# One weight block of a decode kernel brought as sixteen uneven small transfers instead of eight even ones

## The chip, the cores and the metric

The kernel runs on one core of one Trainium2 chip. The metric is the device time of one execution in microseconds. Three runs of the kernel before gave 675.16, 675.23 and 676.45 us, so the median is 675.23 us.

## The reference

The model is one decode step with two parts on the same input `x` (2 rows of 448), mixed by a gate:

```python
def reference(A_x, A_k_cache, A_v_cache, A_wq, A_wo, B_x, B_w1, B_w2, gate_w):
    ...
    x = A_x
    g = _sigmoid((x * gate_w).sum(-1, keepdims=True))
    a = _A_ref(x, A_k_cache, A_v_cache, A_wq, A_wo)   # attention, 16 heads of 256, 4096 cached keys, then wo
    b = _B_ref(x, B_w1, B_w2)                         # relu(x @ w1) @ w2, 448 -> 1792 -> 448
    return g * a + (1 - g) * b
```

All is float32. The two caches hold 2 x 16 x 4096 x 256 values each and are read once; they are 268 MB of the 289.6 MB that the kernel reads.

## The kernel before

The work is cut into 32 units, one for each batch row and head. A unit's keys and values are one transfer of 128 rows of 65,536 bytes, which goes into one of three slots in on-chip memory. All large loads are issued from the SyncE queue (SP), in program order: `wq` and two units ahead of the loop, thirty units in the loop (L126 to L131), each when its slot is free, and then the function `late`. TensorE makes a unit's scores, VectorE the maximum and the weighted sums of the values, ScalarE the exponentials.

`late` (L141) brings the last weights, in this order on one queue:

- `w1` (128 rows of 23,296 bytes, one transfer) into slot 2, as soon as the last unit there has been used up;
- `w1x`, the part of w1 that lies apart: the last 448 columns of w1's 128 rows. It is packed as 64 rows of 3,584 bytes and goes to partitions 0 to 63, in eight transfers of 8 rows (L144 to L146). A transfer's rows lie four partitions apart;
- `w2` (128 rows of 25,088 bytes);
- `wo` in five transfers of 128 rows into slot 0 (14, 10, 4, 3 and 1 blocks of 448 columns, `CUTS`), as soon as slot 0 is free.

TensorE waits for w1 and for all of `w1x` in front of the first product of the second part (L336), then for w2 (L357), and then for each piece of wo in front of the blocks that it holds (L375). The last product of the program uses the last blocks of wo. After it VectorE copies the result (`res`, L397) and SP stores it (`out`, L402).

A transfer is carried by several of the core's 16 DMA engines, each with its share of the rows and, behind them, a 4-byte write that raises the transfer's semaphore; a semaphore at 16 says that all has landed. In the text below such a write is called a mark. DMA engines take their shares in the order in which the transfers were issued.

Of the kernel before, what the change touches and what calls it, by code (L numbers as in the profile page):

```python
# [8 lines left out]
P, HP = 128, 64  # L9
G = 4  # L10
R = P // G
SLOTS = 3
NB = 2
ENGINES = ("tensor", "vector", "scalar", "gpsimd", "sync")


class Program:
# [6 lines left out]
    def __init__(self, nc):  # L24
        self.nc = nc
        self.code = {e: [] for e in ENGINES}
        self.count = dict.fromkeys(ENGINES, 0)

# [11 lines left out]
    def emit(self, block, sems):  # L40
        def run(name):
            def body(e):
                seen = {}
                for kind, a, b in self.code[name]:
                    if kind == "loop":
                        with e.Fori(0, a) as i:
                            b(e, i)
                        continue
                    for who, n in b:
                        if seen.get(who, 0) < n:  # L50
                            e.wait_ge(sems[who], n)
                            seen[who] = n
                    if kind == "op":
                        a(e).then_inc(sems[name], 1)
                    else:
                        a(e)
            return body

        for name in ENGINES:
            getattr(block, name)(run(name))  # L60


def take(e, sem, n=1):
    e.wait_ge(sem, n)
    e.sem_inc(sem, -n)  # L65


def gated_mix_decode(nc, xg, kv, wq, w1, w1x, w2, wo, out):
# [13 lines left out]
    RB = R // B  # L82
    HB = H // NB
    UB = U // NB
    HH = HB // G
# [5 lines left out]
    def sbuf(name, *shape):  # L91
        return nc.alloc_sbuf_tensor(name, [*shape], F32).ap()

    def bank(name, n=CW):
        return nc.alloc_psum_tensor(name, [P, n], F32).ap()

    NO = NB * HH * J
    CUTS = (0, NO - 18, NO - 8, NO - 4, NO - 1, NO)
    TAIL = 8
    names = [*ENGINES, "xg", "w1x", "w2", *(f"wo{k}" for k in CUTS[1:]), "query", "score", "top", "prob", "room",  # L100
             *(f"land{s}" for s in range(SLOTS)), *(f"free{s}" for s in range(SLOTS)), "out"]
    sem = {n: nc.alloc_semaphore(n) for n in names}
    land = [sem[f"land{s}"] for s in range(SLOTS)]
    free = [sem[f"free{s}"] for s in range(SLOTS)]
    pr = Program(nc)
    pe, dve, act, pool, sp = ENGINES

# [8 lines left out]
    def load(s, src, signal, lo=0, hi=None):  # L116
        hi = src.shape[1] if hi is None else hi
        return lambda e: e.dma_start(slot[s][:, lo:hi], src[:, lo:hi]).then_inc(signal, 16)  # L118
# [15 lines left out]

    W1, WX = w1.shape[1], w1x.shape[2]
    w1_sb, w1x_sb = slot[2][:, :W1 + WX], slot[2][:, W1:W1 + WX]
    w2_sb = slot[2][:, W1 + WX:W1 + WX + NF * D]

    def late(e):  # L141
        take(e, free[2])
        load(2, w1, land[2])(e)
        for k in range(8):  # L144
            o = k // 4 * 4 * 8 + k % 4
            e.dma_start(w1x_sb[o:o + 4 * 7 + 1:4], w1x[k]).then_inc(sem["w1x"], 16)  # L146
        e.dma_start(w2_sb, w2).then_inc(sem["w2"], 16)
        take(e, free[0])
        for lo, hi in zip(CUTS, CUTS[1:]):
            load(0, wo, sem[f"wo{hi}"], lo * D, hi * D)(e)  # L150
        take(e, free[1])

    pr.raw(sp, late)

    ident = sbuf("ident", P, P)
# [56 lines left out]
    W = 2 * KF * DH  # L212
    WQ = wq.shape[1] // NB
    wide = sbuf("wide", P, CW)
    pr.raw(pe, lambda e: take(e, land[2], 16))
    busy = [(), ()]
    for i in range(NB):
        w = slot[2][:, i * WQ:(i + 1) * WQ]
        for c in range(KC):
            for g in range(G):  # L220
                r = rows_of(c, g // 2)
                at = g * W + c * CW if c < KF else G * W + g % 2 * CW
# [7 lines left out]
        for s in range(2):  # L230
            dst = qt.rearrange("p t (i g s b) -> p i s t g b", i=NB, g=G, s=2)[:, i, s]
            src = pt[:, ::RB].rearrange("p (s t g b) -> p s t g b", s=2, t=T, g=G)[:, s]
# [100 lines left out]
    hs = wide[:, :FG]  # L333
    hr = sbuf("hr", P, NF, R)
    ph, pt = pw[3], pw[2]
    pr.raw(pe, lambda e: (take(e, land[2], 16), e.wait_ge(sem["w1x"], 16 * 8)))  # L336
    half = (W1 + WX // 2) // 2
    for c in range(KC):
        for g in range(G):
            j, i = divmod(g, 2)  # L340
            at = i * half + (j * KF + c if c < KF else 2 * KF + i * j) * FG
# [26 lines left out]
    n = NO - TAIL  # L368
# [17 lines left out]
    at = 0  # L386
# [80 lines left out]
```

## Time and profile before

| | before |
|---|---|
| median of 3 runs | 675.23 us (675.16 to 676.45) |
| span of the profiled execution | 674.6 us |
| DMA packets, bytes | 6180, 289.66 MB |
| queue of the large loads (q1), share of 16 engines | 99.3% |
| VectorE busy | 341.5 us (51%) |
| TensorE busy | 224.6 us (33%) |
| issue of the eight `w1x` transfers on SP | 5.48 us, from 619.67 |
| landing of the last-but-one piece of wo, which ends TensorE's last wait | 671.59 us |
| result copied, store issued | 672.75, 673.05 us |

The profiled execution has its span and no time of its own beside it; the span lies 0.6 us under the median of the runs. The times in the tables count from the first instruction of the span. The share of a DMA queue is the time that its packets took, over 16 engines and the whole span. In a table of stretches, the column "DMA share" is the same for that stretch: 1.00 is all 16 engines at work, 0.50 is eight. Packets that overlap a little on one engine can lift it over 1.

### The profile page before, as it was taken

What the parts mean: (1) busy time and instruction counts of PE and PEld (TensorE: products, weight loads), DVE (VectorE), ACT (ScalarE), POOL (GpSimd) and SP (SyncE); (2) the same over time, 40 slices, a digit from 0 to 9 for tenths busy, and PEclk for the clock granted to TensorE, in tenths of its full rate; (3) what the DMA queues carried; (4) which work ended last, traced back from release to release, by engine and by line L of the source; (5) the groups of instructions that cost most, each with busy time, mean ns of one, the idle gap of its engine ahead of it and who ended that gap; (6) DMA issues with size and microseconds to landing.
All of it is one profiled execution on the core that took longest, in us unless ns stands there. A gap on an engine that the chain in (4) does not pass through costs nothing. (4 is left out here: it accounts for less than half of the span.)

```text
span 674.6 us, 4166 instructions
## 1 busy us (share of the span) xinstructions
PE 224.6 (33%) x1323; PEld 67.0 (10%) x1323; DVE 341.5 (51%) x571; ACT 59.7 (9%) x121; POOL 0.7 (0%) x6
## 2 busy tenths in 40 slices
PE   0643221333332123333322333333222333321277
PEld 0210000001001000100100010010001001000022
DVE  0006566544556664455566545455665544657652
ACT  0020001001000100100010010000001001000010
POOL 0000000000000000000000000000000000000000
PEclk9975567667655666765566676665567666556688
DMA  9999999999999999999999999999999999999997
GB/s 381 428 435 436 436 435 435 435 435 435 435 431 435 435 435 435 435 431 435 435 435 435 435 435 435 435 435 435 435 435 435 435 431 427 435 427 435 400 444 316
DMA packets 6180, 289.66 MB, mean 429 GB/s; under 512 B 992, under 2 KB 1120, under 8 KB 1440
## 3 DMA queue, kind: packets, MB, share of 16 engines
q1 hardware_dynamic: 6032, 289.60, 99.3%
q8 instruction: 3, 0.05, 0.0%
q10 hardware_dynamic: 144, 0.01, 0.0%
q14 instruction: 1, 0.01, 0.0%
HBM read 289.54 MB, written 0.06 MB: 429 GB/s over the span
## 5 line engine op out<-in xcount | busy, mean ns | idle before, releaser
L274 DVE SCALAR_TENSOR_TENSOR slot<-slot,prob 128x1024 f32<-128x1024 f32 x256 | 295.9, 1222 | 65.1 <-DVEq L65 65.1
L251 PE MATMUL ps<-slot,query 128*32 128x512 f32 x1024 | 190.8, 909 | 404.4 <-PEq L65 404.3
L270 DVE TENSOR_REDUCE nm<-ps 128x1024 f32 (+1 forms) x32 | 39.2, 1225 | 230.8 <-DVEq L65 230.8
L251 PEld LDWEIGHTS ps<-slot,query 128*32 128x32 f32 x1024 | 54.7, 158 | 539.1 <-issue 539.0
L263 ACT ACTIVATE prob<-ps,nm 128x1024 f32<-128x1024 f32 x32 | 35.6, 1113 | 385.0 <-ACTq L65 384.9
L263 ACT ACT_TABLE_LOAD x10 | 12.8, 1283 | 163.4 <-ACTq L65 163.4
L274 DVE DVE_READ_ACCUMULATOR slot<-slot,prob (+1 forms) x256 | 21.3, 83 | 0.0
L187 PE MATMUL pw<-slot,xr 128*32 128x512 f32 (+3 forms) x96 | 12.9, 671 | 1.3 <-DMA slot<-in_w1x 1.3
L176 DVE COPY xr<-xg_sb 128x128 f32<-128x128 f32 x4 | 0.6, 224 | 18.0 <-DMA xg_sb<-in_xg 18.0
L187 PE MATMUL pw<-xg_sb,xr 128*128 128x1 f32 (+1 forms) x8 | 1.9, 352 | 21.2 <-DVE xu L178 21.2
L187 PE MATMUL acc<-slot,ot 128*32 128x448 f32 x48 | 7.2, 661 | 2.3 <-DMA slot<-in_wo 2.2
L258 ACT ACTIVATE query<-qt 128x2 f32 (+1 forms) x32 | 6.2, 193 | 0.0
L263 ACT ACTIVATION_READ_ACCUMULATOR prob<-ps,nm (+1 forms) x32 | 6.2, 193 | 0.0
L187 PE MATMUL acc<-slot,hr 128*32 128x448 f32 x28 | 4.9, 810 | 2.0 <-DMA slot<-in_w 2.0
L190 PE MATMUL pw<-ident,nm 128*16 128x128 f32 x2 | 0.7, 328 | 12.6 <-DVEq L324 12.6
L187 PEld LDWEIGHTS pw<-xg_sb,xr 128*128 128x128 f32 (+1 forms) x8 | 1.8, 321 | 21.2 <-DMA xg_sb<-in_xg 21.2
L187 PEld LDWEIGHTS pw<-slot,xr 128*32 128x32 f32 (+1 forms) x96 | 2.8, 122 | 9.9 <-issue 7.7
L190 PE MATMUL pw<-ident,wide 128*128 128x128 f32 x11 | 1.9, 288 | 2.4 <-ACT wide L193 2.4
L310 DVE TENSOR_TENSOR os<-ov,pw 128x128 f32<-128x128 f32 x2 | 0.6, 287 | 4.0 <-PE pw L187 4.0
L318 DVE COPY ot<-pw 128x256 f32<-128x256 f32 x4 | 1.5, 420 | 2.0 <-PE pw L187 2.0
L391 DVE COPY wide<-acc 128x448 f32<-128x448 f32 x1 | 0.6, 624 | 3.1 <-PE pw L187 3.1
L187 PE MATMUL pw<-slot,ot 128*32 128x112 f32 x64 | 2.0, 261 | 0.2 <-DMA slot<-in_wo 0.2
(42 smaller groups left out, 20.9 us busy)
## 6 DMA issues: line engine op xcount, KB each, us to landing
slot<-in_wq SPq DMA_DIRECT2D x1, 7168.0 KB, 19.4
slot<-in_w SPq DMA_DIRECT2D x1, 3136.0 KB, 29.9
slot<-in_wo SPq DMA_DIRECT2D x1, 3136.0 KB, 21.2
slot<-in_w SPq DMA_DIRECT2D x1, 2912.0 KB, 28.2
slot<-in_wo SPq DMA_DIRECT2D x1, 2240.0 KB, 26.1
slot<-in_wo SPq DMA_DIRECT2D x1, 896.0 KB, 27.8
slot<-in_wo SPq DMA_DIRECT2D x1, 672.0 KB, 28.9
slot<-in_kv SPq DMA_DIRECT2D x32, 38.4
```

Source lines behind the costliest of these rows:

```text
L176: pr.op(dve, lambda e, g=g: e.tensor_copy(xr[:, :, g], xg_sb[:, :, :B, None].to_broadcast([P, KC, B, RB])))
L187: return pr.op(pe, lambda e: e.matmul(out, lhs, rhs, start=start, stop=stop), *after)
L190: return pr.op(pe, lambda e: e.transpose(out, src, ident), *after)
L251: m = e.matmul(ps[g * R:(g + 1) * R, c * CW:(c + 1) * CW], query[s][:, t:t + 1].to_broadcast([P, R]), slot[s][:, lo:lo + CW], start=(t == ...
L258: e.activation(query[s], qt[:, :, bass.ds(u, 1)].rearrange("p t o -> p (t o)"), AF.Copy).then_inc(sem["query"], 1)
L263: e.activation(prob, ps, AF.Exp, bias=nm[:, bass.ds(u, 1)], accum_out=ls[:, bass.ds(u, 1)]).then_inc(sem["prob"], 1)
L270: e.tensor_reduce(nm[:, bass.ds(u, 1)], ps, axis=AX.X, op=ALU.max, negate=True).then_inc(sem["top"], 1)
L274: m = e.scalar_tensor_tensor(v, v, 1.0, prob, op0=ALU.mult, op1=ALU.mult, accum_out=ov[:, bass.ds(u, 1), j])
L310: t = pr.op(dve, lambda e: e.tensor_tensor(os, ov[:, us], wp[:, :UB, None].to_broadcast([P, UB, J]), op=ALU.mult), t)
L318: t = pr.op(dve, lambda e, hh=hh: e.tensor_copy(ot[:, i, hh], po[:, hh * B * J:(hh + 1) * B * J].rearrange("p (b j o) -> p j b o", j=J, o= ...
L391: t = pr.op(dve, lambda e: e.tensor_copy(a_sb, acc), t)
```

## The change

`w1x` is kept as 128 half rows of 448 values (1,792 bytes) and brought in sixteen transfers. They come in pairs that share sixteen half rows between them: 15 and 1, 14 and 2, 13 and 3, down to 8 and 8. Each half row goes to the same place in on-chip memory as before. TensorE waits for sixteen transfers instead of eight. The list on the host that packs the half rows follows the same order.

```diff
+MOVE = 448
+STAIRS = [(half, b, *part) for half in range(2) for b in range(4)
+          for n in (15 - 4 * half - b,) for part in ((0, n), (n, 16))]
...
-    W1, WX = w1.shape[1], w1x.shape[2]
+    W1, WX = w1.shape[1], 2 * MOVE
...
-        for k in range(8):
-            o = k // 4 * 4 * 8 + k % 4
-            e.dma_start(w1x_sb[o:o + 4 * 7 + 1:4], w1x[k]).then_inc(sem["w1x"], 16)
+        at = 0
+        for half, b, lo, hi in STAIRS:
+            e.dma_start(w1x_sb[4 * lo + b:4 * (hi - 1) + b + 1:4, half * MOVE:(half + 1) * MOVE],
+                        w1x[at:at + hi - lo]).then_inc(sem["w1x"], 16)
+            at += hi - lo
...
-    pr.raw(pe, lambda e: (take(e, land[2], 16), e.wait_ge(sem["w1x"], 16 * 8)))
+    pr.raw(pe, lambda e: (take(e, land[2], 16), e.wait_ge(sem["w1x"], 16 * len(STAIRS))))
...
-    w1x = np.concatenate([w1[:HP, -MOVE:], w1[HP:, -MOVE:]], 1)
-    w1x = w1x.reshape(2, 8, 4, -1).transpose(0, 2, 1, 3).reshape(8, 8, -1)
+    w1x = w1[:, -MOVE:].reshape(2, HP, MOVE)
+    w1x = np.concatenate([w1x[half, 4 * lo + b:4 * (hi - 1) + b + 1:4] for half, b, lo, hi in STAIRS])
```

The only queue whose instructions differ is SP's. Before, this stands between the loop's end and the pieces of wo (`slot<-in_w` is w1 ahead of `w1x` and w2 behind it; 8x896 is rows x values):

```order
L118 DMA slot<-in_w 128x5824
L146 DMA slot<-in_w1x 8x896 x8
L147 DMA slot<-in_w 128x6272
L118 DMA slot<-in_wo 128x6272
L118 DMA slot<-in_wo 128x4480
```

In that place the changed kernel has (its line numbers are larger by 3 to 5):

```order
L121 DMA slot<-in_w 128x5824
L149 DMA slot<-in_w1x 15x448
L149 DMA slot<-in_w1x 1x448
L149 DMA slot<-in_w1x 14x448
L149 DMA slot<-in_w1x 2x448
L149 DMA slot<-in_w1x 13x448
L149 DMA slot<-in_w1x 3x448
...
L149 DMA slot<-in_w1x 9x448
L149 DMA slot<-in_w1x 7x448
L149 DMA slot<-in_w1x 8x448 x2
L152 DMA slot<-in_w 128x6272
L121 DMA slot<-in_wo 128x6272
```

Nothing is moved past anything else: the sixteen transfers stand where the eight stood, and w2 and wo are issued behind eight more transfers.

More of the change, by code (lines that the diff above doesn't have):

```diff
@@ L448 @@
     w1 = np.concatenate([full, last], 2).reshape(P, -1)
-    MOVE = 448
-    w1x = np.concatenate([w1[:HP, -MOVE:], w1[HP:, -MOVE:]], 1)
-    w1x = w1x.reshape(2, 8, 4, -1).transpose(0, 2, 1, 3).reshape(8, 8, -1)
+    w1x = w1[:, -MOVE:].reshape(2, HP, MOVE)
+    w1x = np.concatenate([w1x[half, 4 * lo + b:4 * (hi - 1) + b + 1:4] for half, b, lo, hi in STAIRS])
     w1 = w1[:, :-MOVE]
```

## The prediction

> **What bounds the kernel now.** I read the DMA part of the page first, to see whether the queue of the large loads ever rests.
>
> ```profile
> GB/s 381 428 435 436 436 435 435 435 435 435 435 431 435 435 435 435 435 431 435 435 435 435 435 435 435 435 435 435 435 435 435 435 431 427 435 427 435 400 444 316
> DMA packets 6180, 289.66 MB, mean 429 GB/s; under 512 B 992, under 2 KB 1120, under 8 KB 1440
> ...
> q1 hardware_dynamic: 6032, 289.60, 99.3%
> ...
> q10 hardware_dynamic: 144, 0.01, 0.0%
> ```
>
> It does not: q1 fills 99.3% of sixteen engines, at a steady 435 GB/s, so 27.2 GB/s on each engine. The time is that of the bytes, and what an edit of the order can win is only what is lost at the two ends. Next the chain that ended last, for the end:
>
> ```profile
> 642.65 28.93 DMA slot<-in_wo
> 671.59 0.04 issue
> 671.63 1.10 PE pw L187 x32
> 672.73 0.02 issue
> 672.75 0.27 DVE res L397
> ```
>
> The last-but-one piece of wo lands at 671.59, TensorE's last products take 1.10 us, then come the copy and the store. A piece has landed when the latest of its engines has, so the question is which engine is latest, and by how much. The stretches at the end show it:
>
> ```profile
> 669.60:669.80 0.20, 0.20 (x4) 0.00 (x0) 0.00 (x0) 0.00 (x0) 0.00 (x0) 1.00 1.03 421
> 669.80:670.00 0.20, 0.20 (x5) 0.01 (x2) 0.00 (x0) 0.00 (x0) 0.00 (x0) 1.00 0.84 341
> 670.00:670.20 0.20, 0.20 (x8) 0.20 (x10) 0.00 (x0) 0.00 (x0) 0.00 (x0) 1.00 0.71 296
> 670.20:670.40 0.20, 0.20 (x16) 0.20 (x12) 0.03 (x1) 0.00 (x0) 0.00 (x0) 1.00 0.56 224
> 670.40:670.60 0.20, 0.20 (x17) 0.20 (x13) 0.20 (x1) 0.00 (x0) 0.00 (x0) 1.00 0.61 242
> 670.60:670.80 0.20, 0.20 (x17) 0.20 (x10) 0.20 (x1) 0.00 (x0) 0.00 (x0) 1.00 0.75 296
> 670.80:671.00 0.20, 0.20 (x10) 0.01 (x2) 0.19 (x1) 0.00 (x0) 0.00 (x0) 1.00 0.50 188
> 671.00:671.20 0.20, 0.20 (x10) 0.16 (x8) 0.00 (x0) 0.00 (x0) 0.00 (x0) 1.00 0.28 108
> 671.20:671.40 0.20, 0.20 (x8) 0.00 (x0) 0.00 (x0) 0.00 (x0) 0.00 (x0) 1.00 0.19 72
> 671.40:671.60 0.20, 0.04 (x4) 0.00 (x0) 0.00 (x0) 0.00 (x0) 0.00 (x0) 1.00 0.10 36
> 671.60:671.80 0.20, 0.17 (x8) 0.17 (x12) 0.00 (x0) 0.00 (x0) 0.00 (x0) 1.00 0.07 27
> ```
>
> The last two columns are the DMA share and GB/s; a share times 16 is the number of engines still at work. All sixteen work until 669.8. Then some end at once (0.56 is nine engines), most of the others about 1 us later (0.28 near 671.1), three go on past 671.2 (0.19), and one works on alone until about 671.8 (0.07). From 1.6 engines at 671.4 to 671.6, of which one works all the time, the other two end some 0.06 us into that stretch, 0.3 us ahead of the last.
>
> The step of 1 us is `w1x`. The packets under 512 bytes are counted by kind: forty transfers of 128 rows (wq, 32 units, w1, w2, five of wo) leave 16 marks each, 640; the input on q10 is 144 packets (128 rows and 16 marks), the store of 128 rows of 448 bytes as many; of 992 there remain 64, so each of the eight `w1x` transfers left 8 marks: eight engines with one row each. Eight rows of 3,584 bytes at 27.2 GB/s are 1.05 us on each of those engines, and nothing on the other eight. I call them the first eight and the second eight.
>
> Is the last engine one of the first eight?
>
> ```profile
> 648.07 0.16 PEld L187 LDWEIGHTS pw<-slot,xr 128*32 128x32 f32 x8 [2.19 <-DMA slot<-in_w1x]
> ...
> 655.12 1.30 PE L187 MATMUL acc<-slot,hr 128*32 128x448 f32 x8 [1.96 <-DMA slot<-in_w]
> ...
> slot<-in_w SPq DMA_DIRECT2D x1, 3136.0 KB, 29.9
> ```
>
> Some engine of the first eight delivered its last `w1x` row at 648.07 only, and still had its sixteenth of w2 to carry: 200,704 bytes, 7.38 us, so until about 655.4. All of w2 was there at 655.12. The 0.3 us are scatter between data and mark; no room is left for an engine that is later. So the last one is of the first eight. The two that end 0.3 us ahead of it I take for second-eight engines: only seven or so ended early (nine were left at 670.3), though eight have no `w1x`, and one in the middle group may be late as well.
>
> **The change, part by part.** *Cost of a small packet.* q1 took 99.3% of 16 x 674.6 us, 10,718 us; 289.60 MB at 27.2 GB/s are 10,650 us; the rest over 6,032 packets is 11 ns each. The rounding of the three figures puts it between 8 and 14. A half row is then 0.066 + 0.011 us and its mark 0.011, together 0.088 us; an old row with its mark 0.132 + 0.022, together 0.154, and an engine's eight rows 1.23 us.
>
> *Who carries what now.* I take a transfer of n rows to use n engines, from the first on, one row each, as the 8-row transfers did. Counting the sixteen transfers, engine e of the first eight (0 to 7) gets 16 - e half rows, engine e of the second eight (8 to 15) gets 15 - e: 16 down to 9, and 7 down to 0, together 128. The trace has only transfers of 8 and 128 rows and so can't show it for 15 or 13. [...]
>
> So engine 0 needs 16 x 0.088 = 1.41 us (0.18 more than now), engine 2 breaks even, engine 7 needs 0.79 (0.44 less). In the second eight the added time runs from 7 x 0.088 = 0.62 us down to none.
>
> *What it does to the latest landing.* The rows do not say which of the first eight the last engine is. Its change lies between -0.44 and +0.18, in the mean -0.13 us. But the two behind it stand at -0.3 and are raised by 0.088 times zero to seven; for two different places among eight the larger of the two is five on average, so the later one reaches -0.3 + 0.44 = +0.14. The latest of the three therefore ends near +0.1 us; at best (both late ones at the end of the stairs) -0.3, at worst +0.32. What the first engine gives up is handed to engines that have lag of their own.
>
> *Behind the landing.* A later landing passes on in full, 1.10 us of products wait for it. An earlier one is held up by what TensorE has in front:
>
> ```profile
> 671.04 0.40 PE L187 MATMUL pw<-wide,fold 128*32 128x112 f32 x8
> ...
> 671.63 0.97 PE L187 MATMUL pw<-slot,ot 128*32 128x112 f32 x32 [0.19 <-DMA slot<-in_wo]
> ```
>
> It was idle for 0.19 us only. The products ahead of these wait for earlier pieces of wo, which come sooner by the same engine, so part of more than 0.19 can still be had.
>
> *Issue on SP.* Eight more transfers:
>
> ```profile
> 619.28 0.34 SPq L118 DMA_DIRECT2D slot<-in_w  x1
> 619.67 5.48 SPq L146 DMA_DIRECT2D slot<-in_w1x  x8
> 625.19 0.44 SPq L147 DMA_DIRECT2D slot<-in_w  x1
> 641.33 2.23 SPq L118 DMA_DIRECT2D slot<-in_wo  x5
> ```
>
> At 5.48 / 8 = 0.685 us each, sixteen take 10.96 us, and w2's issue ends at 631.1 instead of 625.6. Nobody waits: w2 landed at 655.1 and needs 7.4 us, so its latest engine began near 647.7 and, with the 2 us over which engines are spread at the end, the earliest near 645.7. The wo issues wait for their slot until 641.33. The cover is 14.6 us; it would be gone only if an issue took 1.6 us, and each 0.1 us beyond that would cost 1.6. I take nothing. TensorE's wait for `w1x` shifts by some tenths; behind it 1.96 us are idle before w2 (row above), which hide that.
>
> Sum: 0.1 us on 675.23, so **675.3 us**; the span of 674.6 becomes 674.7. Its own range is 674.9 to 675.6. A gain or loss counts from 0.2%, 1.35 us, which is about what a measurement of this kernel can tell from no change; the three runs themselves spread over 1.3 us.
>
> **The rivals.** *The stairs fit the lag* (0.20): the last engine stands at 5 to 7, the two behind it near 15. Then the latest landing is one of those two, at -0.3 plus next to nothing: 675.0 us. The rows leave this open; for it speaks that nothing bars it, against it that three engines must all stand well. Perfect levelling has its bound in the table: the shares from 669.8 on add up to 4.61, times 0.2 us are 0.92 us of full work, so all engines could end at 670.7, 1.1 us sooner than now. That is less than 1.35 us: no form of this mechanism is faster by 0.2%.
>
> *Engines in each other's way at the destination* (0.26). All 128 half rows still go to partitions 0 to 63, but 28 of them are now carried by the second eight, and the first eight also bring rows to each other's partitions. If two engines that write close partitions at once share one way in, each such half row takes twice 0.066 us, and the owner loses as much. For an engine with 9 to 16 half rows the loss lies between none and 16 x 0.066 = 1.05 us; about half of the rows are aimed at another engine's place, so I take 0.5 us. It decides once the late engine meets more than four such rows. On 675.23 that is 675.7 us, at the far end (0.32 + 1.05) 676.6. The trace has no transfer of this kind, and 27.2 GB/s on each engine fits a limit on either side of it. [...]
>
> *Uneven transfers are not spread* (0.04). If a transfer of an odd number of rows were put on one engine, that one would get the 64 half rows of the eight odd transfers and one of each of the other eight: 72 x 0.088 = 6.3 us instead of 1.23. It would be the last by far: an on-time engine ends near 671.1, 0.7 us ahead of the last, so 5.1 - 0.7 = 4.4 us are lost, 679.6 us, slower. The even split of the 8-row transfers speaks against it.
>
> **How the numbers follow.** The forecast has 0.47, the three rivals 0.20, 0.26 and 0.04, something unseen 0.03. Slower by over 0.2%: the uneven case (0.04), the upper end of the second rival together with a badly placed late engine (0.10), scatter between executions (one of three runs of before stands 0.18% above the median) and the unseen, 0.22 in all. Faster by over 0.2% has no mechanism and keeps 0.06 for scatter. Within: 0.72. The range, 674.8 to 676.6 us, takes in the forecast, the fitting stairs and nearly all of the second rival.
>
> **What would show it.** If the count of engines is right, the page has 6,308 packets, 1,056 of them under 512 bytes (128 marks where 64 were), 1,312 under 2 KB, and SP issues `w1x` in about 11 us. With uneven transfers on one engine there would be about 72 marks. If the levelling is right, the shares from 669.8 on fall without the step at 670.2 and three engines or so still end last; their sum stays near 4.6. If engines get in each other's way, the sum grows, and TensorE's wait for `w1x` ends later than 648.1 by half a us or more. The landing that ends TensorE's last wait should lie between 671.3 and 671.9. The forecast is wrong if the time moves by over 0.4 us.

## The result, and the profile after

Over 13 runs the changed kernel took 676.44 us in the median (676.03 to 678.71), the kernel before 675.48 us over 13 runs (675.10 to 676.76). The ratio is 1.0016, with a 95% interval of 1.0009 to 1.0024: about 1.1 us slower. The spread within each kernel is as large as that, so beside most ratios I also give the fastest run; here the two fastest stand 0.93 us apart.

The page of the changed kernel, DMA part and the chain that ended last:

```profile
DMA packets 6308, 289.66 MB, mean 429 GB/s; under 512 B 1056, under 2 KB 1312, under 8 KB 1568
...
q1 hardware_dynamic: 6160, 289.60, 99.3%
...
641.09 30.82 DMA slot<-in_wo
671.91 0.04 issue
671.95 1.10 PE pw L192 x32
673.05 0.02 issue
673.07 0.27 DVE res L402
```

The packets are 128 more, 64 of them marks, as many as n engines for n rows give. The path at the end has the same pieces; the last-but-one piece of wo lands at 671.91 instead of 671.59. The timeline of SP in the changed kernel, and then TensorE's wait for `w1x`:

```profile
619.54 11.97 SPq L149 DMA_DIRECT2D slot<-in_w1x  x16
631.56 0.45 SPq L152 DMA_DIRECT2D slot<-in_w  x1
639.76 3.34 SPq L121 DMA_DIRECT2D slot<-in_wo  x5
```

```profile
648.86 0.16 PEld L192 LDWEIGHTS pw<-slot,xr 128*32 128x32 f32 x8 [3.25 <-DMA slot<-in_w1x]
```

The sixteen issues take 12 us, and w2's issue behind them is done at 632.0, some 13 us ahead of the time at which w2 is wanted. The wait for `w1x` ends 0.8 us later than before.

The span is only 0.4 us longer (675.0), but the two profiled executions did not come to this place alike. The DMA packets that started between 20 and 640 us, of the kernel before and then of the changed one:

```profile
DMA packets 4622, 268.08 MB, mean 432 GB/s; under 512 B 511, under 2 KB 511, under 8 KB 511
```

```profile
DMA packets 4639, 268.45 MB, mean 433 GB/s; under 512 B 512, under 2 KB 512, under 8 KB 512
```

The changed kernel's execution was ahead by 0.37 MB, up to 0.85 us of streaming (packets of 64 KB make this coarse), before anything that the change touches had moved. So the difference of the spans is too small a measure. The stretch in which `w1x` and w2 move, 644 to 656 us, shows the loss by itself, again before and then changed:

```profile
DMA packets 360, 5.21 MB, mean 434 GB/s; under 512 B 96, under 2 KB 96, under 8 KB 160
```

```profile
DMA packets 473, 4.86 MB, mean 405 GB/s; under 512 B 160, under 2 KB 288, under 8 KB 288
```

Before, the queue runs at its full 434 GB/s through the eight small transfers. Now it moves 0.35 MB less in the same 12 us, 0.8 us at 435 GB/s. I use this row as a measure in the runs below: 5.21 MB is no loss, and each 0.1 MB less is 0.23 us lost on the mean engine. It is a coarse one: two runs below that are no slower than the kernel before have 5.10 and 5.12 MB.

The end of the changed kernel, in the same stretches as before:

```profile
669.80:670.00 0.20, 0.20 (x6) 0.04 (x2) 0.00 (x0) 0.00 (x0) 0.00 (x0) 1.00 0.74 305
670.00:670.20 0.20, 0.20 (x4) 0.00 (x0) 0.00 (x0) 0.00 (x0) 0.00 (x0) 1.00 0.61 251
670.20:670.40 0.20, 0.20 (x6) 0.07 (x6) 0.00 (x0) 0.00 (x0) 0.00 (x0) 1.00 0.66 269
670.40:670.60 0.20, 0.20 (x12) 0.20 (x14) 0.00 (x0) 0.00 (x0) 0.00 (x0) 1.00 0.65 260
670.60:670.80 0.20, 0.20 (x20) 0.20 (x12) 0.08 (x1) 0.00 (x0) 0.00 (x0) 1.00 0.57 224
670.80:671.00 0.20, 0.20 (x20) 0.20 (x12) 0.20 (x1) 0.00 (x0) 0.00 (x0) 1.00 0.60 233
671.00:671.20 0.20, 0.20 (x18) 0.17 (x6) 0.20 (x1) 0.00 (x0) 0.00 (x0) 1.00 0.43 170
671.20:671.40 0.20, 0.20 (x9) 0.00 (x0) 0.14 (x1) 0.00 (x0) 0.00 (x0) 1.00 0.24 90
671.40:671.60 0.20, 0.20 (x10) 0.16 (x8) 0.00 (x0) 0.00 (x0) 0.00 (x0) 1.00 0.10 36
671.60:671.80 0.20, 0.20 (x8) 0.00 (x0) 0.00 (x0) 0.00 (x0) 0.00 (x0) 1.00 0.12 45
671.80:672.00 0.20, 0.05 (x5) 0.05 (x8) 0.00 (x0) 0.00 (x0) 0.00 (x0) 1.00 0.10 36
672.00:672.20 0.20, 0.20 (x12) 0.20 (x16) 0.00 (x0) 0.00 (x0) 0.00 (x0) 1.00 0.03 9
```

The step is flatter, as stairs should make it. But between 671.4 and 672.0 one to two engines are still at work alone (0.10 to 0.12 of sixteen), and the last ends after 672.0. The levelling took place, and the end is no earlier.

### The profile page after: what moved, and what is told of

The parts are those of the page before. It is cut to its first block, busy times and chain, and to the rows that moved or that the text cites. A ratio compares the mean times of both kernels' runs of the same rounds, so it can differ in the third digit from the quotient of the medians.

```text
span 675.0 us, 4174 instructions
## 1 busy us (share of the span) xinstructions
PE 219.9 (33%) x1323; PEld 67.0 (10%) x1323; DVE 341.5 (51%) x571; ACT 59.8 (9%) x121; POOL 0.7 (0%) x6
## 2 busy tenths in 40 slices
DMA packets 6308, 289.66 MB, mean 429 GB/s; under 512 B 1056, under 2 KB 1312, under 8 KB 1568
## 5 line engine op out<-in xcount | busy, mean ns | idle before, releaser
L256 PE MATMUL ps<-slot,query 128*32 128x512 f32 x1024 | 185.9, 888 | 408.8 <-PEq L68 408.7
L192 PE MATMUL pw<-slot,xr 128*32 128x512 f32 (+3 forms) x96 | 14.7, 755 | 2.3 <-DMA slot<-in_w1x 2.3
L192 PE MATMUL acc<-slot,hr 128*32 128x448 f32 x28 | 3.2, 541 | 1.1 <-ACT hr L198 1.1
## 6 DMA issues: line engine op xcount, KB each, us to landing
slot<-in_wo SPq DMA_DIRECT2D x1, 672.0 KB, 30.8
```

The source lines that it names most:

```text
L192: return pr.op(pe, lambda e: e.matmul(out, lhs, rhs, start=start, stop=stop), *after)
L256: m = e.matmul(ps[g * R:(g + 1) * R, c * CW:(c + 1) * CW], query[s][:, t:t + 1].to_broadcast([P, R]), slot[s][:, lo:lo + CW], start=(t == ...
```

## The experiments

Two theories were at hand. The first was the prediction's second rival: a row that an engine brings to another engine's place holds up both. An engine's own place is where the kernel before has it bring rows, counted row by row as in the prediction; a row brought elsewhere is called a visit. No run shows which engine writes where. The second: many small transfers cost by themselves. Each ratio below is to the kernel before, run beside it on the same chip.

**Even half rows, own places.** The changed kernel's transfers and packets, but 8 half rows in each transfer, so that, by this count, all go to the first eight engines and each to its own place.

```diff
-STAIRS = [(half, b, *part) for half in range(2) for b in range(4)
-          for n in (15 - 4 * half - b,) for part in ((0, n), (n, 16))]
+STAIRS = [(half, b, *part) for half in range(2) for b in range(4) for part in ((0, 8), (8, 16))]
```

> Sixteen transfers of 8 half rows: the changed kernel's packets and number of transfers, but no row on the second eight engines and none to another engine's place. Theory (engines in each other's way at the destination cost the time of the change): only eight more small packets and eight more marks per engine of the first eight, 16 x 0.088 instead of 1.23 us, so before + 0.1 to 0.2 us, and w2's rows keep the even pace that they have before (stretch 644 to 656 us moves as many bytes). Rival (the many small transfers and marks cost it): before + 0.9 us, as the changed kernel.

Measured: 676.91 us against 675.69, ratio 1.0017 (1.0008 to 1.0027), fastest 676.12 against 675.11. The stretch and the wait for `w1x`:

```profile
DMA packets 475, 4.91 MB, mean 409 GB/s; under 512 B 160, under 2 KB 288, under 8 KB 288
```

```profile
648.88 0.20 PEld L191 LDWEIGHTS pw<-slot,xr 128*32 128x32 f32 x8 [4.10 <-DMA slot<-in_w1x]
```

My theory missed: with no visit at all, this kernel loses as much as the changed one, and shows the same signs. Sixteen transfers of small rows on one engine cost about 1 us. What it is in them that costs, the rows or the marks, this run does not say.

**Other places.** The kernel before with its eight transfers of 8 rows, but to partitions 64 to 127. The theory assumes that the second eight engines are bringing w2's rows there at the same time.

```diff
-            e.dma_start(w1x_sb[o:o + 4 * 7 + 1:4], w1x[k]).then_inc(sem["w1x"], 16)
+            e.dma_start(w1x_sb[HP + o:HP + o + 4 * 7 + 1:4], w1x[k]).then_inc(sem["w1x"], 16)
...
-            r = rows_of(c, j * (1 - i))
+            r = rows_of(c, max(i, j))
```

> The eight transfers of 8 rows of the kernel before, but to partitions 64 to 127; TensorE reads the block there, so the result is the whole one. Counts per engine, packets and issue are those of before. Theory: each of the first eight engines now brings its 28.7 KB through the way in of an engine of the second eight, which is bringing w2 there; both lose 1.05 us at most, so before + 0.6 to 1.1 us, and bytes in 644 to 656 us drop. Rival (small packets or the uneven counts cost it, destination does not matter): before + 0.0.

Measured: 676.84 us against 675.69, ratio 1.0023 (1.0014 to 1.0032), fastest 676.35, 1.24 over the fastest of before.

```profile
DMA packets 343, 4.79 MB, mean 399 GB/s; under 512 B 96, under 2 KB 96, under 8 KB 160
```

Packets, transfers and engines are those of before, only the place differs, and 0.42 MB are lost in the stretch: 0.97 us, where the theory's estimate was 1.05 us at most (eight rows of 3,584 bytes at 27.2 GB/s). The trace keeps each DMA packet with its start, size and time, and the packets agree: the 3,584-byte rows, 0.140 us each before, take up to 0.282 us, twice as long, and 24 rows of w2, 0.93 us each before, take up to 1.71 us. That is the first theory's sign, rows of both transfers held up; that they meet at one way in is its assumption, the packets show only the times. Both effects are real.

**Sixteen half rows in a transfer.** Every engine has 8 half rows and 8 marks, and the second eight visit the first.

```diff
-STAIRS = [(half, b, *part) for half in range(2) for b in range(4)
-          for n in (15 - 4 * half - b,) for part in ((0, n), (n, 16))]
+STAIRS = [(half, b, 0, 16) for half in range(2) for b in range(4)]
```

> Eight transfers of 16 half rows to partitions 0 to 63: every engine has 8 half rows, and the second eight bring theirs to the places of the first eight. Theory: the first eight save half their rows and lose as much to the visitors; the second eight, with two late engines 0.3 us behind the last, get 8 x (0.088 + 0.066) = 1.2 us, so before + 0.9 us. Rival (place does not matter): first eight 0.5 us earlier, second eight 0.7 us later, the late two at -0.3 + 0.7, so before + 0.4 us. If small packets cost the time of the change, half of its extra packets give before + 0.5 us.

Measured: 676.51 us, ratio 1.0009 (1.0000 to 1.0018), fastest 676.10, 1.0 over before.

```profile
DMA packets 474, 4.88 MB, mean 407 GB/s; under 512 B 160, under 2 KB 288, under 8 KB 288
```

The ratio lies between what the two expected and can't tell them apart; the bytes and the fastest run speak for the visits, and so does a run below in which eight marks on an engine, without visits, lose nothing.

**One level transfer.** The 128 half rows in a single transfer over all partitions: 8 half rows and one mark for each engine, all, as the theory takes it, in their own places.

```diff
-        for k in range(8):
-            o = k // 4 * 4 * 8 + k % 4
-            e.dma_start(w1x_sb[o:o + 4 * 7 + 1:4], w1x[k]).then_inc(sem["w1x"], 16)
+        e.dma_start(w1x_sb[:, :WX // 2], w1x).then_inc(sem["w1x"], 16)
...
-            at = i * half + (j * KF + c if c < KF else 2 * KF + i * j) * FG
-            r = rows_of(c, j * (1 - i))
+            at = i * half + (j * KF + c if c < KF else 2 * KF) * FG
+            r = rows_of(c, j)
```

> The same 128 half rows in one transfer over all 128 partitions (the block's second half on partitions 64 to 127, where TensorE reads it): every engine 8 half rows, all to its own place, one mark each. Theory: first eight 0.6 us earlier, second eight 0.6 us later, the late two of these at -0.3 + 0.6, so before + 0.3 us, and w2's rows at an even pace. Rival (levelling in itself decides, late engines of the second eight do not matter): before - 0.5 us.

Measured: 675.80 us, ratio 0.9999 (0.9990 to 1.0009), fastest 675.43, 0.3 over before.

```profile
DMA packets 371, 5.10 MB, mean 425 GB/s; under 512 B 48, under 2 KB 176, under 8 KB 176
```

The end of its profile:

```profile
669.60:669.80 0.20, 0.20 (x4) 0.00 (x0) 0.00 (x0) 0.00 (x0) 0.00 (x0) 1.00 0.87 341
669.80:670.00 0.20, 0.20 (x6) 0.14 (x8) 0.00 (x0) 0.00 (x0) 0.00 (x0) 1.00 0.37 144
670.00:670.20 0.20, 0.20 (x15) 0.20 (x12) 0.00 (x0) 0.00 (x0) 0.00 (x0) 1.00 0.33 134
...
671.40:671.60 0.20, 0.15 (x8) 0.15 (x12) 0.00 (x0) 0.00 (x0) 0.00 (x0) 1.00 0.07 27
```

Levelling without visits and with few marks costs nothing that can be measured, and wins nothing: no gain was measured. The interval reaches down to 0.7 us of gain, so it does not exclude the 0.5 us that levelling alone was to win; the fastest run, above that of before, speaks against it. The end of the profile shows what levelling leaves: most engines stop together around 669.8, but about five (0.33 of sixteen) work on past 670, and one is at work until near 671.6, with no more bytes to carry than the others. Why these are late is not shown.

**Two half rows to a mark.** To part small rows from marks: sixteen half rows on each of the first eight engines, as with even halves, but in eight transfers, so 8 marks.

```diff
-            e.dma_start(w1x_sb[o:o + 4 * 7 + 1:4], w1x[k]).then_inc(sem["w1x"], 16)
+            e.dma_start(w1x_sb[o:o + 4 * 7 + 1:4].rearrange("r (h n) -> r h n", h=2),
+                        w1x[k].rearrange("h r n -> r h n")).then_inc(sem["w1x"], 16)
...
-    w1x = w1x.reshape(2, 8, 4, -1).transpose(0, 2, 1, 3).reshape(8, 8, -1)
+    w1x = w1x.reshape(2, 8, 4, 2, -1).transpose(0, 2, 3, 1, 4).reshape(8, 2, 8, -1)
```

> Sixteen half rows for each of the first eight engines as in the run with even halves, but in eight transfers of 8 x 2 half rows, so 8 marks per engine instead of 16. Theory (an engine can land only a mark about every 0.2 us, and rows queued behind too many marks are held up): 8 x 0.2 = 1.6 us of marks beside 1.2 us of rows, as in the kernel before, so before + 0.1 us, and w2's rows at their even pace. Rival (128 small rows cost it, by their size or by how they lie in main memory): before + 0.9 us, as with sixteen transfers of 8 half rows.

Measured: 675.39 us against 676.03, ratio 0.9994 (0.9985 to 1.0003), fastest 675.21 against 675.17.

```profile
DMA packets 422, 5.17 MB, mean 431 GB/s; under 512 B 96, under 2 KB 224, under 8 KB 224
```

```profile
647.47 0.16 PEld L188 LDWEIGHTS pw<-slot,xr 128*32 128x32 f32 x8 [2.54 <-DMA slot<-in_w1x]
```

The same 128 small rows, half the marks: the loss is gone (packets under 2 KB beyond those under 512 bytes are 128 in the stretch here and with even halves). So the small rows by themselves do not cost it.

The packets show where the time goes instead. With even halves the last row of `w1x` has moved at 646.70 us and the wait for it ends 2.18 us later; with two rows to a mark these are 646.74 us and 0.73 us, and in the kernel before 647.32 us and 0.75 us. What comes late is the marks behind the rows. And with even halves sixteen rows of w2, as many as two for each of the eight engines, take up to 1.61 us; here none takes over 0.94 us. A mark never comes without a transfer of its own in these runs, so they can't tell its write from anything else that one more transfer brings to an engine; what is said of marks below holds with this limit.

**Two semaphores.** Even halves again, with the marks on two semaphores by turns.

```diff
-                        w1x[at:at + hi - lo]).then_inc(sem["w1x"], 16)
+                        w1x[at:at + hi - lo]).then_inc(sem["w1y" if lo else "w1x"], 16)
...
-    pr.raw(pe, lambda e: (take(e, land[2], 16), e.wait_ge(sem["w1x"], 16 * len(STAIRS))))
+    pr.raw(pe, lambda e: (take(e, land[2], 16), e.wait_ge(sem["w1x"], 16 * 8), e.wait_ge(sem["w1y"], 16 * 8)))
```

> The run with even halves again (sixteen transfers of 8 half rows), with the transfers' marks on two semaphores by turns instead of one. Theory (the limit is per engine): before + 0.9 us, as with one. Rival (all marks queue for one semaphore): half the queue for each, before + 0.1 to 0.3 us.

Measured: 677.63 us against 676.03, ratio 1.0023 (1.0013 to 1.0033), fastest 676.35, 1.2 over before.

```profile
DMA packets 474, 4.88 MB, mean 407 GB/s; under 512 B 160, under 2 KB 288, under 8 KB 288
```

A second semaphore does not help: the 0.1 to 0.3 us of the rival lie outside the interval, so the marks do not queue for one semaphore.

**Quarter rows.** Thirty-two transfers of 8 quarter rows: 32 marks on each of the first eight engines.

```diff
-        for k in range(8):
-            o = k // 4 * 4 * 8 + k % 4
-            e.dma_start(w1x_sb[o:o + 4 * 7 + 1:4], w1x[k]).then_inc(sem["w1x"], 16)
+        for k in range(32):
+            o, q, n = k // 4 % 8 // 4 * 4 * 8 + k // 4 % 4, k % 4, WX // 4
+            e.dma_start(w1x_sb[o:o + 4 * 7 + 1:4, q * n:(q + 1) * n], w1x[k]).then_inc(sem["w1x"], 16)
...
```

> Thirty-two transfers of 8 quarter rows (896 bytes), own places, 32 marks on each of the first eight engines. Theory: 32 x 0.2 = 6.4 us of marks beside 1.8 us of rows; with 16 marks some 2 us of marks too many cost 0.9 us, so with 4.6 too many before + 3 to 4 us. Rival (only the 11 ns of each packet): 48 more packets on each of the engines than before, before + 0.5 us. SP issues until about 642 us, still ahead of the time at which w2's first row is wanted (645).

Measured: 680.20 us against 676.03, ratio 1.0065 (1.0051 to 1.0078), so 4.4 us (3.4 to 5.3), a little over what was expected.

```profile
DMA packets 695, 4.21 MB, mean 350 GB/s; under 512 B 280, under 2 KB 536, under 8 KB 536
```

```profile
619.19 21.47 SPq L146 DMA_DIRECT2D slot<-in_w1x  x32
```

```profile
652.15 0.20 PEld L187 LDWEIGHTS pw<-slot,xr 128*32 128x32 f32 x8 [6.88 <-DMA slot<-in_w1x]
```

```profile
641.27 24.92 DMA slot<-in_wo
666.20 0.04 issue
666.24 1.72 PE acc L187 x8
```

The issues are not late: SP is through with them at 640.7, and the first quarter row moves at 644.5. From 16 to 32 marks on an engine the last landing of `w1x` moves from 648.88 to 652.15: 3.27 us for 16 marks, 0.20 us each. The time moves by 4.4 - 1.15 = 3.2 us. That fits, but it is no second measure of the same thing: the chain that ended last leaves the DMA at 666.20 here, when the first piece of wo lands, and from there on goes through TensorE's products (so it does with sixteen half rows, from 662.89 on). Rows of 896 bytes are not tried without more marks.

**Stairs of full rows.** Back to the changed kernel's shape, with fewer marks: 15 and 1 to 12 and 4 full rows, 64 marks, no engine over 8.

```diff
-STAIRS = [(half, b, *part) for half in range(2) for b in range(4)
-          for n in (15 - 4 * half - b,) for part in ((0, n), (n, 16))]
+STAIRS = [(b, *part) for b in range(4) for n in (15 - b,) for part in ((0, n), (n, 16))]
...
```

> Stairs of full rows of 3,584 bytes: 15 and 1, 14 and 2, 13 and 3, 12 and 4, eight transfers, 64 marks. Counts per engine are 8, 7, 6, 5, then 4 for engines 4 to 11, then 3, 2, 1, 0; 32 of the 64 rows go to another engine's place, as many bytes as 64 half rows (56 in the changed kernel). Theory (marks cost the change its time): no engine has more marks than before, so only levelling (+ 0.3 us or so, as in the run with one level transfer) and visits are left, before + 0.3 to 0.6 us. Rival (visits cost it): before + 0.9 us or more, and w2's rows stretched as in the changed kernel.

Measured: 676.33 us against 676.03, ratio 1.0007 (0.9998 to 1.0016), fastest 675.82, 0.65 over before.

```profile
DMA packets 343, 4.80 MB, mean 400 GB/s; under 512 B 96, under 2 KB 96, under 8 KB 160
```

```profile
647.79 0.16 PEld L191 LDWEIGHTS pw<-slot,xr 128*32 128x32 f32 x8 [3.81 <-DMA slot<-in_w1x]
```

The stretch loses as much as in the changed kernel, without its marks: these are the visits. `w1x` is there 1.1 us earlier than in the changed kernel. The ratio puts the time 0.5 us over before (-0.1 to 1.1), inside the 0.3 to 0.6 us of the theory; the fastest runs, 0.65 us apart, lie just above that, and the stretch is as the rival expected.

**The same stairs with twice the marks,** and the changed kernel once more beside it.

```diff
-          for n in (15 - 4 * half - b,) for part in ((0, n), (n, 16))]
+          for n in (15 - b,) for part in ((0, n), (n, 16))]
```

> The stairs of full rows again (15 and 1 down to 12 and 4), with each row cut into two half rows that come in transfers of their own: sixteen transfers, the same bytes and the same visits on each engine, twice the marks (16 on engine 0, 8 on engines 4 to 11). Theory (marks and visits both cost): the full-row stairs were 0.5 us over before; engine 0 to 3 now have 16 to 10 marks, some 2 us of marks too many at most, so before + 0.8 to 1.0 us, as the changed kernel. Rival (with uneven counts only visits matter): before + 0.5 us again.

> The changed kernel itself, on the same chip as the other two: before + 0.9 to 1.0 us.

Measured: 676.32 us against 675.67 for the stairs, ratio 1.0006 (0.9997 to 1.0015), fastest 675.93, 0.8 over before. The changed kernel: 676.54 us, ratio 1.0010 (1.0002 to 1.0019), fastest 676.08, 1.0 over before. The stretch, first of these stairs, then of the changed kernel:

```profile
DMA packets 473, 4.86 MB, mean 405 GB/s; under 512 B 160, under 2 KB 288, under 8 KB 288
```

```profile
DMA packets 471, 4.81 MB, mean 401 GB/s; under 512 B 160, under 2 KB 288, under 8 KB 288
```

So with stairs, 64 more marks add at most 0.2 us by the ratios and the fastest runs (each ratio is uncertain by 0.6 us), less than I expected; where visits already hold the engines up, the marks behind them seem to cost little more. The packets say the same. Over those that start between 640 and 657 us, the time beyond what their sizes take undisturbed adds up, over all engines, to 10.2 us with the stairs of full rows, 9.8 us with twice the marks and 10.1 us in the changed kernel (9.4 us with even halves, 18.5 us with other places). How the loss of the changed kernel divides between the two is only bounded: about half of it or more is there without the extra marks.

**Less moved.** The other direction, from the term in the prediction that the last engine is one of the first eight and 0.3 us behind two others: 320 of the 448 columns moved, the rest in w1.

```diff
+            if c == KF and i * j:
+                stay, far = FG - WX // 2, rows_of(c, 1)
+                t = mm(ph[g * R:(g + 1) * R, :stay], flat(xr[far, c, g]), w1_sb[far, W1 - stay:W1], False, False)
+                t = mm(ph[g * R:(g + 1) * R, stay:FG], flat(xr[r, c, g]), w1_sb[r, W1 + WX // 2:W1 + WX], False, True, t)
+                continue
...
-    MOVE = 448
+    MOVE = 320
```

> The eight transfers of 8 rows of the kernel before with 320 of the 448 columns moved (rows of 2,560 bytes); the other 128 columns stay in w1, one more product on TensorE. The first eight engines carry 4,096 bytes less in all (0.15 us), the second eight 4,096 bytes more. If the last engine is one of the first eight and the two behind it, 0.3 us earlier, are of the second eight, all three end together: before - 0.15 us. Rival (a late engine of the second eight is last): before + 0.15 us. The time of the runs can hardly tell the two, the DMA shares at the end of the profile can.

Measured: 675.93 us against 675.67, ratio 0.9999 (0.9991 to 1.0008), fastest 675.31 against 675.11. It does not beat the kernel before; 0.15 us either way can't be read from these runs. The shares at the end of its profile (0.23, 0.14 and 0.05 in the stretches of 0.2 us from 671.0 on), which were to tell the two apart, do not settle it either. No version here beat the kernel before.

## Why the prediction was right, and where it was wrong

*Who carries what* was right: the 6,308 packets with 1,056, 1,312 and 1,568 under the three sizes are the numbers that n rows on n engines give, the one-row transfer included. The rival with uneven transfers on one engine is out. So is any cost on SP: 11.97 us of issue, where 10.96 were reckoned, which is well inside the cover.

*The bound on a gain* was right. No gain was measured, neither by the stairs nor by one level transfer. The direction of the forecast held, slower, and the ratio is within 0.2% (its interval reaches 0.24%). But the forecast's own range of 674.9 to 675.6 did not hold; the changed kernel's fastest run is 676.03. The time moved by 1.1 us (0.6 to 1.6), which is past the 0.4 us that the prediction gave as the sign of being wrong. The wider range, 674.8 to 676.6, holds the 676.44 only because it was drawn to take in the second rival. That the direction came out is luck: the 0.1 us was to come from late engines that are given more rows, and one level transfer, which gives them more, showed no loss that could be measured; what was measured came from the marks and the visits. Two terms were too small: the price of a mark, and the visits, which the sum took at nothing.

*The price of a mark* failed. The prediction took 11 ns for it, from the time that packets took on their engines. That is what a mark occupies (9 ns in the packets of before), not what it makes the engine wait: from 16 to 32 marks, each puts off the last landing by 0.20 us, eighteen times as much, and from 8 to 16 (two half rows to a mark, then even halves) the wait moves from 647.47 to 648.88, 0.18 us each; the ratios 0.9994 and 1.0017, from different chips and each uncertain by 0.6 us, lie 1.55 us apart. Eight marks in 1.2 us of rows, as before, show no loss, and 16 small rows with 8 marks show none either. At 0.20 us each, eight would take 1.6 us, an estimate; but in the kernel before marks of `w1x` landed until 648.03, when its last row had moved at 647.32, and no row of w2 took over 0.93 us, so some were outstanding while rows moved at their full pace. The sum of before's packet times could therefore not reveal the price. The prediction did read a sign of it in another way: it took 648.07 for the time at which the last row of `w1x` was delivered, but that row had moved at 647.32, and the rest was the marks. That each engine waits for its own marks agrees with the two semaphores, since a second one did not help (ratio 1.0023, beside 1.0017 with one); what holds a mark back for 0.2 us was not shown.

*Engines in each other's way* was the second rival, with a chance of 0.26. Its loss is shown: the kernel before with another destination loses 0.97 us on the mean engine in the stretch, against 1.05 us worked out. For the stairs of full rows it costs some 0.5 us, which is what the rival took. The rows that went to partitions 64 to 127 took up to 0.282 us instead of 0.140, the twice that the rival took for two engines on one way in. That there is such a way in, and which engines meet there, was its assumption and was not shown. The forecast weighed this as less likely than no contention, on the ground that 27.2 GB/s per engine fits either limit; the runs show that the destination alone can cost time: with only the place changed, the stretch moved 4.79 MB instead of 5.21.

*The signs that were to tell the rivals apart* did not. A later wait for `w1x` (648.86 for 648.07) and a larger sum of shares at the end (4.85 for 4.61 from 669.8 on) both came, as the second rival would have them, and the landing that ends TensorE's last wait came at 671.91, just past the 671.3 to 671.9 of the forecast. But even halves, without any visit, gave the same wait (648.88). Had I stopped at the trace, I would have put all of the loss down to the visits.

*The late engines*: levelling was expected to leave the end where it was, since what the first eight give up goes to engines that lag. One level transfer bears that out (0.9999). The prediction's reading that the last engine is one of the first eight holds in the packets of before, on other figures than its own. The q1 packets of before fall into sixteen chains in which one starts as the last one ends (4 ns ahead of that in the median), and eight of the chains have eight rows of `w1x` each. With a chain taken for an engine, the engine that moved the last row of `w1x` is also the last to end w2, at 654.74, and the next, 0.29 us ahead of it, carried no `w1x`. Which of the first eight it is was left open, and is so still.

## What to carry to other kernels

Where one queue is full, a small transfer is not paid for by its bytes or packets alone. Count the completion writes on each DMA engine, and put several rows behind one of them; in this kernel 16 on an engine in 1.2 us of rows cost 1 us and 32 cost 4.4 us, while 8 cost nothing that could be measured. Before levelling bytes over engines, see where the rows go (the same eight transfers to other partitions cost 1.2 us by the fastest runs here), and see which engines are late: work that is taken off one late engine and handed to another won nothing here.

## What the runs showed of the hardware that I had not expected

- From 16 to 32 completion writes on an engine, each with its transfer, the last landing came 0.20 us later for each (3.27 us in all), and rows of the next transfer were held up: with 16, sixteen rows of w2 took up to 1.61 us; with 8 behind as many small rows, none took over 0.94. Spreading them over two semaphores did not help (ratio 1.0023, beside 1.0017 with one).
- The same transfers to partitions 64 to 127 instead of 0 to 63 cost 1.2 us by the fastest runs, with the queue's rate in the stretch down from 434 to 399 GB/s.
- Uneven transfers of 15 rows down to 1 are issued nearly as fast as 8-row ones: 0.75 us each over all sixteen, beside 0.685.
